# Pinning one VectorE instruction, the fallback's mask, to the middle of phase one

## The chip, the cores and the metric

The kernel runs on one core of a Trainium2 chip. The core has five engines with an instruction stream each: TensorE (PE in the profile, its weight loads are PEld), VectorE (DVE), ScalarE (ACT), GpSimd (POOL) and SyncE (SP), which here only issues DMAs. The metric is the device time of one execution in microseconds (us). The kernel before took 1256.52 us, the median of three runs (1255.74 to 1257.02).

## What is computed

Two independent layers work on inputs of 2048 rows by 1024, and their outputs stand side by side in the result (2048 by 2048, bf16).

Part A is a diagonal complex state-space layer. Its recurrence over the 2048 rows is a complex scan per state:

```python
Lam_bar = jnp.exp(dt * Lam)
B_bar = ((Lam_bar - 1.0) / Lam)[:, None] * Bmat
Bu = jnp.einsum('bld,pd->blp', x + 0j, B_bar)
for t in range(L):
    h = Lam_bar[None, :] * h + Bu[:, t, :]
y = 2.0 * jnp.einsum('blp,dp->bld', hseq, Cmat).real + x * Dskip[None, None, :]
```

Part B is attention with a recurrent memory: 64 segments of 32 rows, each with 8 memory rows in front, 32 heads of 128. The memory of a segment is the first 8 rows of the output of the segment before.

```python
for s in range(n_seg):
    h = jnp.concatenate([mem, xs], axis=1)
    q, k, v = (jnp.einsum('btd,dhe->bhte', h, W) for W in (Wq, Wk, Wv))
    scores = jnp.where(mask, q @ k.T * scale, -1e9)
    o = jnp.einsum('bhte,hed->btd', softmax(scores) @ v, Wo)
    mem = o[:, :M, :]
    outs.append(o[:, M:, :])
```

The mask lets row i see column j where i < 8 or i >= j.

## The kernel before

**The plan.** The kernel guesses the memory rows of all segments from averages, computes all segments at once, and at the end checks the guess (`check`, line 790). Only if the check fails does a branch run `general`, the fallback, which goes through the 64 segments one after another. With these inputs the branch is not taken. The fallback needs a small mask of its own, `k.fmask` (40 by 2 by 40, f32): plane 0 is the 0/1 mask, plane 1 is (plane 0 - 1) * 1e9, to be added to the scores. Nothing but `general` reads it.

**The stages on TensorE.** Phase one (0 to about 343 us) alternates the value projections of part B (`v_x`: 8 head blocks by 4 quarters of the rows) with the input side of part A (`stage1`: 8 blocks of states by 4 blocks of rows, 32 units numbered n = 4*pc + q). Phase two, to about 486 us, is the output side of part A and the guess. Phase three, to about 1027 us, interleaves the query and key projections with attention. Phase four is the output projection, with the check inside it.

**The start.** Eight matmuls on zeros (`warm`) come first. Then `v_x(0, 0)`, the first 512 rows: four tiles of x (128 rows each) arrive untransposed in `b_xr`; for each tile TensorE makes eight transposes into a PSUM buffer psU (two such buffers), and `turn_x0` copies them into `b_xe`, on VectorE for tiles 0 and 2 and on ScalarE for tiles 1 and 3 (`k.copy("vs"[i % 2], ...)`, line 410; the copy itself shows as L89 on VectorE and L87 on ScalarE). TensorE's order is: transposes of tiles 0 and 1; the products of tiles 0 and 1 with the first 128 columns of Wv; transposes of tile 2; the rest of tiles 0 and 1; transposes of tile 3; the whole product of tile 2 (eight matmuls of 512 columns), then of tile 3, this one into a psU buffer. After that come two small transpositions for part A's parameters (`a_r`) and the memory rows (`a_h`), and the second block's values, `v_x(1, 0)`. All later x chunks come transposed by DMA, issued by SP. The products are copied to `b_vst` (two buffers, mostly by ScalarE) and stored to DRAM by ScalarE's queue.

**A unit of stage 1.** 16 matmuls into psU; VectorE multiplies by a table (L265, which frees the psU buffer), adds (L268), scans (L273) and, after a ScalarE copy, multiplies and adds again (L284, L285, into `a_h`, which SP stores). GpSimd computes the carry into the next unit (L278 to L280). `tables` (L221 to L236) makes the tables for the next block of states, on VectorE and ScalarE.

**Masks.** When the loop reaches n == 12 it calls `masks(k)`, GpSimd's masks for attention (lines 112 to 149), and `check_consts(k)`, which builds `k.skip` and `k.fmask`: three GpSimd instructions for plane 0 (L930, L931, L933) and one VectorE instruction for plane 1 (L934).

**What sets the order.** The program is written in one order, but the framework draws the order on each engine itself, by a modelled schedule in which an instruction may go as soon as its inputs are ready. Semaphores are put in afterwards. Exceptions are named by hand: `keep_in_program_order(ins)` adds an order-only edge from the instruction that was written just before `ins` for the same engine. In phase one every TensorE instruction and every DMA of SP is so pinned (`k.pin`); VectorE, ScalarE and GpSimd are not. From phase two on TensorE is free (`k.pin.remove("PE")`), from phase three on SP too. So an instruction without much to wait for, written at n == 12, can stand far ahead of that place in its engine's stream.

Of the kernel before, what the change touches and what calls it, by code (L numbers as in the profile page):

```python
# [12 lines left out]
ALU = mybir.AluOpType  # L13
# [907 lines left out]
def check_consts(k):  # L921

    V, G = k.V, k.G
    k.skip = k.cst.tile([128, 1], FP32, name="c_skip")
    G.memset(k.skip[:], 0.0)
    for r in (2, NTL - 2, NTL - 1):
        G.affine_select(out=k.skip[:], in_=k.skip[:], compare_op=ALU.not_equal, fill=1.0, base=-r,  # L927
                        pattern=[[0, 1]], channel_multiplier=1)
    k.fmask = k.cst.tile([L, 2, L], FP32, name="f_mask")
    G.memset(k.fmask[:], 1.0)  # L930
    G.affine_select(out=k.fmask[:, 0, :], in_=k.fmask[:, 0, :], compare_op=ALU.is_ge, fill=0.0, base=0,  # L931
                    pattern=[[-1, L]], channel_multiplier=1)
    G.memset(k.fmask[0:M, 0, :], 1.0)  # L933
    V.tensor_scalar(k.fmask[:, 1, :], k.fmask[:, 0, :], 1.0, 1.0e9, ALU.subtract, ALU.mult)  # L934


def steps():
# [31 lines left out]
def kernel_main(tc, A_x, A_Lre, A_Lim, A_Bre, A_Bim, A_Cre, A_Cim, A_logdt, A_Dskip, B_x, B_mem0, B_Wq, B_Wk, B_Wv, B_Wo, out,  # L969
                force=False, dbg=None):  # L970
    with ExitStack() as ctx:
# [16 lines left out]
        with pool("p1x", "right") as p1x, pool("p1", "right", 1) as p1:  # L988
# [28 lines left out]
            for kind, pc, q in order[1:]:  # L1017
# [27 lines left out]
                if n == 12:  # L1045
                    masks(k)
                    check_consts(k)
# [167 lines left out]
```

## Time and profile before

| what | value |
|---|---|
| median of three runs | 1256.52 us |
| the profiled execution | 1256.46 us |
| its span, first to last instruction | 1254.8 us |
| mean granted TensorE clock | 0.997 |
| TensorE busy, 0 to 343.2 us | 335.38 us |
| TensorE busy, 343.2 to 486 us | 141.91 us |
| TensorE busy, 486 to 1027 us | 540.07 us |
| TensorE busy, 1027 to 1255 us | 221.92 us |
| VectorE busy, 100 to 300 us | 90% in the first half, 91% in the second |
| DMA, mean busy share of its engines, 0 to 100 us | 91% |

"Busy" is the time in which at least one instruction of the engine ran; matmuls are pipelined and their ends are modelled. Lines are of kernel.py; a copy or matmul made through a helper carries the helper's line (L62 for every TensorE instruction of the kernel and every DMA of SP, L89 and L87 for copies), so tiles are told apart by the names of output and input. An arrow in brackets at the end of a timeline line gives how long the engine had been idle before the instruction, and what released it.

### The profile page before, as it was taken

What the parts mean: (1) busy time and instruction counts of PE and PEld (TensorE: products, weight loads), DVE (VectorE), ACT (ScalarE), POOL (GpSimd) and SP (SyncE); (2) the same over time, 40 slices, a digit from 0 to 9 for tenths busy, and PEclk for the clock granted to TensorE, in tenths of its full rate; (3) what the DMA queues carried; (4) which work ended last, traced back from release to release, by engine and by line L of the source; (5) the groups of instructions that cost most, each with busy time, mean ns of one, the idle gap of its engine ahead of it and who ended that gap; (6) DMA issues with size and microseconds to landing.
All of it is one profiled execution on the core that took longest, in us unless ns stands there. A gap on an engine that the chain in (4) does not pass through costs nothing.

```text
span 1254.8 us, 20111 instructions
## 1 busy us (share of the span) xinstructions
PE 1239.3 (99%) x8270; PEld 664.9 (53%) x8342; DVE 667.6 (53%) x1246; ACT 263.7 (21%) x631; POOL 273.3 (22%) x407
## 2 busy tenths in 40 slices
PE   8999999999999999999999999999999999999998
PEld 4444444444455555556566656556565654446444
DVE  3688899998811124666666666666666641001000
ACT  3544344443310000111112121112111210000000
POOL 3112322121322220232222232222322220000000
PEclk8999999999999999999999999999999999999999
DMA  9975524564698929245464544545373279507000
GB/s 247 233 184 136 161 96 121 157 149 135 181 327 251 280 93 277 69 89 128 105 147 105 135 111 105 135 96 122 92 160 92 58 218 211 117 18 152 18 17 27
DMA packets 314744, 174.18 MB, mean 139 GB/s; under 512 B 138648, under 2 KB 300048, under 8 KB 314648
## 3 DMA queue, kind: packets, MB, share of 16 engines
q1 hardware_dynamic: 292552, 146.22, 48.4%
q10 hardware_dynamic: 21072, 23.47, 5.7%
q0 software_dynamic: 1024, 3.17, 0.7%
q8 instruction: 66, 1.08, 0.4%
q14 instruction: 30, 0.25, 0.1%
HBM read 87.47 MB, written 52.19 MB: 111 GB/s over the span
## 4 chain that ended last, share of the span: by engine, by line
PE 98%; POOL 1%; issue 1%; ACT 0%; DVE 0%; POOLq 0%; ACTq 0%
PE psP L62 81%; PE psU L62 9%; PE psS L62 3%; PE psO L62 2%; PE psR L62 2%; POOL b_m L639 0%; POOL a_r L163 0%; ACT b_e L636 0%; POOL maskB L123 0%; POOL maskA L123 0%; POOL maskB L122 0%; DVE b_xe L89 0%; POOL c_skip L927 0%; POOL maskB L129 0%; POOL maskA L122 0%
## 5 line engine op out<-in xcount | busy, mean ns | idle before, releaser
L62 PE MATMUL psP<-b_xe,b_wq 128*128 128x480 bf16 (+1 forms) x1280 | 247.8, 342 | 0.1
L62 PE MATMUL psP<-b_xe,b_wk 128*128 128x480 bf16 (+1 forms) x1280 | 247.7, 343 | 0.0
L62 PE MATMUL psP<-b_wv,b_xe 128*128 128x512 bf16 (+2 forms) x1033 | 225.1, 375 | 5.5 <-DVE b_xe L89 4.9
L639 POOL TENSOR_TENSOR b_m<-b_e,maskB 99x396 bf16<-99x396 bf16 x160 | 139.4, 871 | 335.9 <-ACT b_e L636 335.9
L636 ACT ACTIVATE b_e<-psS 99x396 bf16<-99x396 f32 x176 | 88.0, 500 | 534.5 <-PE psS L62 526.9
L62 PEld LDWEIGHTS <-b_wk 128*128 128x128 bf16 x1280 | 119.3, 98 | 94.5
L62 PEld LDWEIGHTS <-b_xe 128*128 128x128 bf16 x1056 | 102.7, 99 | 125.3 <-DVE b_xe L89 4.6
L62 PEld LDWEIGHTS <-b_wq 128*128 128x128 bf16 x1280 | 118.5, 98 | 88.1
L89 DVE CAST b_k<-psP 128x480 bf16<-128x480 f32 (+1 forms) x192 | 98.1, 532 | 100.6 <-PE psP L62 100.6
L89 DVE CAST b_q<-psP 128x480 bf16<-128x480 f32 (+1 forms) x192 | 98.1, 532 | 93.9 <-PE psP L62 92.1
L62 PEld LDWEIGHTS <-b_ol 128*128 128x128 bf16 x864 | 84.3, 98 | 94.4
L62 PE MATMUL psU<-a_xT,a_bt 128*128 128x512 bf16 x493 | 113.9, 379 | 1.1
L62 PE MATMUL psP<-t,a_hl 128*128 128x512 bf16 x496 | 112.1, 379 | 0.8
L89 DVE CAST b_ost<-psP 128x512 bf16<-128x512 f32 (+1 forms) x17 | 11.5, 676 | 183.4 <-PE psP L62 182.4
L62 PE MATMUL psP<-wo,b_ol 128*128 128x512 bf16 (+1 forms) x440 | 91.9, 364 | 0.4
L62 PE MATMUL psP<-t,b_ol 128*128 128x512 bf16 x408 | 91.7, 379 | 0.4
L87 ACT ACTIVATE b_vst<-psP 128x512 bf16<-128x512 f32 x126 | 72.3, 591 | 80.0 <-PE psP L62 74.5
L278 POOL TENSOR_SCALAR a_tt<-a_pr,a_tabf 128x1 f32<-128x1 f32 x48 | 34.0, 709 | 250.8 <-DVE a_pr L273 250.8
L656 DVE TENSOR_TENSOR b_ob<-psO,b_accR 99x384 bf16<-99x384 f32 x160 | 85.9, 553 | 2.2
L265 DVE TENSOR_TENSOR a_pr<-psU,a_tabf 128x2048 f32<-128x2048 f32 x32 | 73.0, 2282 | 16.3 <-PE psU L62 14.6
L62 PEld LDWEIGHTS <-a_bt 128*128 128x128 bf16 x512 | 49.2, 98 | 57.6
L62 PEld LDWEIGHTS <-a_hl 128*128 128x128 bf16 x512 | 49.1, 98 | 56.6
(198 smaller groups left out, 965.0 us busy)
## 6 DMA issues: line engine op xcount, KB each, us to landing
b_v<-b_vx SPq DMA_DIRECT2D x16, 1064.2 KB
b_wv<-in_B_Wv_dram SPq DMA_DIRECT2D x16, 1024.0 KB
b_on<-b_ob SPq DMA_DIRECT2D x15, 960.0 KB
b_vx<-b_vst ACTq DMA_DIRECT2D x24, 516.0 KB
a_hs<-a_h SPq DMA_DIRECT2D x32, 256.0 KB
b_wog<-in_B_Wo_dram SPq DMA_DIRECT2D x4, 2048.0 KB
b_wq<-in_B_Wq_dram SPq DMA_DIRECT2D x16, 512.0 KB
b_wk<-in_B_Wk_dram SPq DMA_DIRECT2D x16, 512.0 KB
```

The costliest lines, as they stand in the source:

```text
L62: r = f(*a, **kw)
L87: self.S.activation(out, in_, ACT.Copy)
L89: self.V.tensor_copy(out, in_)
L265: V.tensor_tensor(pr[:], u[:].unsqueeze(1).to_broadcast([128, 2, 2, TB]), view(t3, [[TB + 1, 2], [TB + 1, 2], [1, TB]]), ALU.mult)
L278: G.tensor_scalar(tt[:, j:j + 1], w[:, j, TB - 1:TB], t3[:, 1, TB:TB + 1], None, ALU.mult)
L636: k.S.activation(e[:], s[0:GW], ACT.Exp, scale=float(E) ** -0.5, accum_out=self.accE[0:GW, i:i + 1])
L639: k.G.tensor_tensor(m[:, 0:4 * GW].rearrange("p (a b q) -> p a b q", a=2, b=2), e[:], mask[0:GW, :, :].unsqueeze(2).to_broadcast([GW, 2, 2 ...
L656: V.tensor_tensor(self.ob[:, b0:b0 + n, :], o[0:GW, 0:n, 0:E], r.unsqueeze(2).to_broadcast([GW, n, E]), ALU.mult)
```

## The change

The one VectorE instruction of `check_consts` is handed to `keep_in_program_order`. What was written before it for VectorE is the last instruction of `stage1` for n == 12, the add into `a_h` (L285); the order edge comes from there. The instruction itself, its operands and the GpSimd instructions that it reads from stay as they are.

```diff
@@ -931,7 +931,7 @@
     G.affine_select(out=k.fmask[:, 0, :], in_=k.fmask[:, 0, :], compare_op=ALU.is_ge, fill=0.0, base=0,
                     pattern=[[-1, L]], channel_multiplier=1)
     G.memset(k.fmask[0:M, 0, :], 1.0)
-    V.tensor_scalar(k.fmask[:, 1, :], k.fmask[:, 0, :], 1.0, 1.0e9, ALU.subtract, ALU.mult)
+    k.tc.keep_in_program_order(V.tensor_scalar(k.fmask[:, 1, :], k.fmask[:, 0, :], 1.0, 1.0e9, ALU.subtract, ALU.mult))
```

## The prediction, made before the change was run

> **What bounds the kernel now.** First the page: busy time by engine, the slices, the chain that ended last, the costliest groups.
>
> ```profile
> PE 1239.3 (99%) x8270; PEld 664.9 (53%) x8342; DVE 667.6 (53%) x1246; ACT 263.7 (21%) x631; POOL 273.3 (22%) x407
> ...
> PEclk8999999999999999999999999999999999999999
> ...
> PE 98%; POOL 1%; issue 1%; ACT 0%; DVE 0%; POOLq 0%; ACTq 0%
> ...
> L62 PE MATMUL psP<-b_wv,b_xe 128*128 128x512 bf16 (+2 forms) x1033 | 225.1, 375 | 5.5 <-DVE b_xe L89 4.9
> ```
>
> TensorE is busy 1239.3 of 1254.8 us and carries 98% of the chain; only 15.5 us are not matmul. So an edit on VectorE counts only where TensorE waits for VectorE. The last line names such a place (4.9 us), and the clock row is below full in the first slice alone. Next, who waited for whom (total, times, longest, in us):
>
> ```profile
> DVE f_mask L934 <- POOL f_mask L933: 8.3, 1, 8.3
> ...
> PE psP L62 <- DVE b_xe L89: 4.9, 1, 4.9
> ```
>
> The instruction that is pinned is itself a wait: VectorE stood 8.3 us before it. TensorE's only long wait in the whole span is for a VectorE copy of b_xe. The order of time in the first 32 us shows that they are one event:
>
> ```profile
> 6.37 0.42 DVE L210 CAST a_jf<-a_k 128x513 f32<-128x513 int32 x1
> ...
> 10.86 0.61 PE L62 MATMUL psU<-ident,b_xr 128*128 128x128 bf16 x8
> ...
> 11.50 1.02 ACT L87 ACTIVATE b_xe<-psU 128x1024 bf16<-128x1024 bf16 x1 [0.72 <-PE psU L62]
> ...
> 15.09 0.18 DVE L934 TENSOR_SCALAR f_mask<-f_mask 40x40 f32<-40x40 f32 x1 [8.30 <-POOL f_mask L933]
> 15.19 0.68 DVE L89 COPY b_xe<-psU 128x1024 bf16<-128x1024 bf16 x1
> 15.79 0.68 DVE L89 CAST b_vst<-psP 128x512 bf16<-128x512 f32 x1
> 15.92 0.13 PEld L62 LDWEIGHTS <-b_xe 128*128 128x128 bf16 x2 [4.63 <-DVE b_xe L89]
> 16.32 3.19 PE L62 MATMUL psP<-b_wv,b_xe 128*128 128x512 bf16 x7 [4.86 <-DVE b_xe L89]
> ...
> 19.31 2.69 PE L62 MATMUL psU<-b_wv,b_xe 128*128 128x512 bf16 x8
> ...
> 21.93 0.18 PE L62 MATMUL psR<-ident,a_r 24*128 24x24 bf16 x1
> ```
>
> GpSimd builds its masks from 5.17 to 15.06 us. VectorE holds the mask instruction until the last of them, and the copy of x tile 2 into b_xe is queued behind it. That tile's transposes start at 8.66 and last 0.61 us, so the copy could have run at about 9.3. TensorE finishes the transposes of tile 3 at 11.47 and has nothing until the copy. Last, the clock around the hole (per stretch: busy us of PE, PEld, DVE, ACT, POOL; then PEclk, DMA share, GB/s):
>
> ```profile
> 11.00:11.50 0.50, 0.47 (x9) 0.29 (x6) 0.00 (x0) 0.00 (x0) 0.36 (x5) 1.00 1.10 378
> ...
> 13.50:14.50 1.00, 0.00 (x0) 0.00 (x0) 0.00 (x0) 0.00 (x0) 0.86 (x8) 0.80 0.95 213
> 14.50:15.50 1.00, 0.00 (x0) 0.00 (x0) 0.41 (x2) 0.00 (x0) 0.49 (x4) 0.50 2.23 175
> ...
> 16.30:19.50 3.20, 3.18 (x8) 1.21 (x8) 0.16 (x1) 0.00 (x0) 0.00 (x0) 0.50 1.06 223
> ...
> 21.00:22.00 1.00, 1.00 (x7) 0.34 (x6) 0.00 (x0) 0.00 (x0) 0.00 (x0) 1.00 1.27 289
> ```
>
> The hole costs twice: the wait, and a clock that falls to 0.50 in it and is back only near 20.8 us.
>
> **What the Trainium skill says.** "TensorE: Matmul & The Clock Gate", Part 1: an idle window of about 3.4 us halves the clock and about 3.4 us of work restores it. The trace agrees: the fall is inside the 4.4 us hole, the recovery some 4.9 us after the restart at 15.9. Same page, Architectural detail: VectorE's queue is strict FIFO. The copy behind the mask shows that. "SBUF — State Buffer", two separate sides: VectorE and GpSimd can block each other on a shared port pair. The copy will now run while GpSimd builds masks, so this matters; the same copy at 5.76 us, beside GpSimd's work, took 692 ns against 675 at 15.19 with GpSimd idle. I take no loss.
>
> **The change, part by part.** The pin adds an order edge: the mask comes after the VectorE instruction traced before it, which is the sum into a_h (L285) of the 13th stage-1 unit (n = 12).
>
> (a) *The wait goes.* The record at 16.32 has seven of eight matmuls; eight half-rate ones of 427 ns (3.19 us for 7 and a bit) back from 19.31 begin at 15.89. So TensorE's hole is 11.46 to 15.89 = 4.43 us. What is late next? Tile 2's copy would end at about 9.35 + 0.69 = 10.0, before 11.46. Tile 3's copy, on ScalarE, ends at 12.52 and is needed only after tile 2's eight matmuls, at 13.2. The psU buffer for tile 3's product is freed by tile 2's copy at 10.0. So the hole is gone: 4.43 us.
>
> (b) *The slow clock goes.* The 16 matmuls for tiles 2 and 3 run from 15.89 to 21.93 = 6.04 us. At full rate 32 such matmuls take 6.91 us on the chain, 0.216 each: 3.46 us. Saved 2.58 us. Sum (a)+(b): 7.01 us; the a_r transposition would start at 11.46 + 3.46 = 14.92 instead of 21.93.
>
> (c) *What now comes 7 us earlier must be there.* DMA does not move with TensorE: it is near saturation until 60 us. Bytes counted from the span's start put the three MB of x tiles and Wv before 11.5 us (the rate falls from 378 to 282 GB/s there), so block 1's Wv, needed at 15.2, has arrived. SP issues the transposed x chunks of b_xe and a_xT back to back; from the GB/s rows I estimate that they land about 15, 24 (a_xT 0), 29, 34, 40, 49 and 54 us. Their uses, 7 us earlier than now, fall at 22.1, 35.9, 39.5, 46.4, 56.7, 60.2 and 67.5. The least slack is about 7 us. Two or three of ScalarE's 516 KB stores fall earlier among them, some 1 MB or 4 us at 240 GB/s: still covered. From 60 us SP's loads follow a_h and buffers, which shift with TensorE. I charge nothing; if the cover fails, 1 to 3 us come back.
>
> (d) *The mask in its new place.* 177 ns on VectorE. GpSimd was done at 15.06, so no wait. Its neighbours now, on VectorE:
>
> ```profile
> 173.09 0.68 DVE L285 TENSOR_TENSOR a_h<-a_n 128x1024 bf16<-128x1024 bf16 x1
> 173.69 2.28 DVE L265 TENSOR_TENSOR a_pr<-psU,a_tabf 128x2048 f32<-128x2048 f32 x1
> ```
>
> Behind it is the product of unit 13, which frees a psU buffer at 175.97; TensorE needs that buffer for unit 15 at 188.73. The cover is 12.8 us against 0.18, and VectorE itself waits for TensorE at 192.38. Cost 0, at most 0.18. If GpSimd's mask work were also moved there (9.9 us ahead of the carries that the scans need), the cover would still hold it. No DMA is moved; SP is passed by nothing.
>
> (e) *After phase one.* Past the first five microseconds TensorE has no other wait over 0.4 us, so the shift should arrive at the end whole.
>
> Sum: the profiled execution, 1256.46 us (span 1254.8 and 1.7 around it), becomes 1249.45, span 1247.8. It lies 0.06 below the median 1256.52, so the median becomes 1249.5.
>
> **Rivals.**
> 1. *A transfer takes the wait's place*: Wv of block 1, or the first store of b_vst, which ScalarE's later copies into that buffer wait for. For: DMA is full. Against: the byte count. Gives back about 2 us: 1251.5.
> 2. *Only the hole goes, the clock is low anyway*, because some 3 us of idleness stay: 4.4 us off, 1252.1. Against: (a) finds no second releaser after 11.46 us.
> 3. *The pin does not do it*: another instruction waiting for GpSimd is placed early on VectorE. Only a_jf reads GpSimd there, and it is already past at 6.79: 1256.5.
> 4. *Slower*: the framework orders unpinned instructions by a modelled schedule; a shift of the start redraws the order in attention, where TensorE is not pinned. Each of 176 score units waits for ScalarE and GpSimd; with 0.08 us more per unit TensorE loses 14 us and the end is 1263.5. It decides from 7.0/176 = 0.04 us per unit. For: 160 mask products of 871 ns stand in that loop. Against: TensorE is 100.00 busy in each 100 us of it, so the order has reserve.
>
> **How the numbers follow.** Forecast 0.80; rivals 0.09, 0.03, 0.03, 0.05. The time is the forecast's: 1249.5. Its own spread is that of the three runs, 0.8 below and 0.5 above, plus 0.18 for (d) and about 0.3 for the copy's start; the range runs on through rival 1: 1248.4 to 1251.8. No change means within 0.2%, 2.5 us, about what a measurement can tell. Faster: forecast and rivals 1 and 2, 0.92; same 0.03; slower 0.05.
>
> **What would show it.** VectorE's 8.3 us wait for f_mask absent; the b_xe copy near 9.4; no TensorE hole at 11.5; clock 1.00 from 12 to 22 us; the a_r transposition near 14.9; L934 near 167 us, with no idle before it; unit 0 of stage 1 near 36.0 instead of 43.0. It is wrong if TensorE waits for a DMA before 70 us, if the clock falls at about 13 us all the same, or if attention shows new waits.

## The result and the profile after

| kernel | median, us | range, us | runs |
|---|---|---|---|
| before | 1256.49 | 1255.74 to 1257.02 | 6 |
| after | 1250.43 | 1249.00 to 1254.56 | 6 |

The ratio is 0.9958, with a 95% interval of 0.9941 to 0.9976. The gain is 6.1 us, where 7.0 was forecast, and the times now spread over 5.6 us, where before they spread over 1.3. The experiments below trace both differences mainly to one wait, and the profiled execution, 1253.39 us (span 1251.6), is one of those that it touched. First the page of the changed kernel: busy time, clock, chain, and the group that had waited for b_xe.

```profile
PE 1241.9 (99%) x8342; PEld 664.0 (53%) x8342; DVE 667.9 (53%) x1246; ACT 263.5 (21%) x631; POOL 273.3 (22%) x407
...
PEclk9999999999999999999999999999999999999999
...
PE 98%; DMA 1%; ACT 1%; POOL 0%; DVE 0%; issue 0%; ACTq 0%
...
L62 PE MATMUL psP<-b_wv,b_xe 128*128 128x512 bf16 (+2 forms) x1048 | 226.1, 375 | 2.7 <-ACT b_vst L87 2.4
```

The clock row has lost its 8. In the chain that ended last GpSimd (POOL) has gone from 1% to 0%, and DMA has come in with 1%. The value projections still wait, but for ScalarE's copy into b_vst, and no longer for VectorE's copy of b_xe. The start in order of time (start, duration, engine, line, work, count; in brackets the idle time before and its releaser):

```profile
8.95 0.69 DVE L89 COPY b_xe<-psU 128x1024 bf16<-128x1024 bf16 x1 [2.16 <-PE psU L62]
10.50 0.61 PE L62 MATMUL psU<-ident,b_xr 128*128 128x128 bf16 x8
...
10.95 1.89 PE L62 MATMUL psP<-b_wv,b_xe 128*128 128x512 bf16 x8
12.67 1.89 PE L62 MATMUL psU<-b_wv,b_xe 128*128 128x512 bf16 x8
...
14.49 0.18 PE L62 MATMUL psR<-ident,a_r 24*128 24x24 bf16 x1
```

The copy of tile 2 runs at 8.95 (before 15.19), the products of tiles 2 and 3 follow the transposes of tile 3 without a hole and at full rate, and the a_r transposition starts at 14.49 instead of 21.93: 7.44 us earlier. Then, from the order of time in the stretch from 20 to 48 us:

```profile
23.73 6.00 SPq L62 DMA_TRANSPOSE b_xe<-in_B_x_dram  x1
...
25.17 0.37 ACTq L493 DMA_DIRECT2D b_vx<-b_vst  x1
...
29.81 0.39 ACTq L493 DMA_DIRECT2D b_vx<-b_vst  x1
...
35.76 1.09 ACT L87 ACTIVATE b_vst<-psP 128x512 bf16<-128x512 f32 x2 [5.37 <-DMA b_vx<-b_vst]
36.41 3.53 PE L62 MATMUL psP<-b_wv,b_xe 128*128 128x512 bf16 x8 [2.40 <-ACT b_vst L87]
...
39.78 3.62 PE L62 MATMUL psU<-a_xT,a_bt 128*128 128x512 bf16 x16
```

ScalarE issues the second store of b_vst, that of `v_x(1, 0)`, at 25.17. The fourth block of values needs the same buffer (there are two), ScalarE stands 5.37 us until the store has landed, the PSUM buffers stay full, and TensorE stands 2.40 us. Unit 0 of stage 1 begins at 39.78, against 43.01 before: of the 7.44 us won, 3.23 are left, which is the difference of the spans (3.2). The chain of waits, shown over 25 to 50 us, has the store in it:

```profile
25.17 10.51 DMA b_vx<-b_vst
...
35.76 0.61 ACT b_vst L87
36.41 3.53 PE psP L62 x8
```

The stretches around it (per stretch: busy us of PE, PEld, DVE, ACT, POOL; PEclk, DMA share, GB/s) show that this wait, too, costs more than its length:

```profile
34.00:35.00 1.00, 0.01 (x1) 0.00 (x0) 0.00 (x0) 0.00 (x0) 0.00 (x0) 1.00 1.14 188
35.00:36.00 1.00, 0.00 (x0) 0.00 (x0) 0.00 (x0) 0.24 (x1) 0.00 (x0) 1.00 1.20 185
36.00:37.00 1.00, 0.59 (x2) 0.25 (x2) 0.00 (x0) 1.00 (x3) 0.00 (x0) 0.68 1.18 201
37.00:38.00 1.00, 1.00 (x3) 0.29 (x2) 0.51 (x1) 1.00 (x3) 0.00 (x0) 0.50 1.28 290
```

The clock falls to 0.50 once more. Eight matmuls take 3.37 us (36.41 to 39.78) where eight at full rate take 1.73: 1.64 us on top of the 2.40. Last, VectorE around the pinned instruction:

```profile
169.85 0.69 DVE L285 TENSOR_TENSOR a_h<-a_n 128x1024 bf16<-128x1024 bf16 x1
170.45 0.19 DVE L934 TENSOR_SCALAR f_mask<-f_mask 40x40 f32<-40x40 f32 x1
170.56 2.27 DVE L265 TENSOR_TENSOR a_pr<-psU,a_tabf 128x2048 f32<-128x2048 f32 x1
```

It stands where the edit put it, with no idle time before it. On VectorE it is the only instruction whose place in the order changed; TensorE, GpSimd and SP have the same order as before, and on ScalarE two neighbours, a copy for the scan (L274) and a copy of products (L87), changed places.

### The profile page after: what moved, and what is told of

Its sections match the earlier page's. It is cut to its first block, busy times and chain, and to the rows that moved or that the text cites. A ratio compares the mean times of both kernels' runs of the same rounds, so it can differ in the third digit from the quotient of the medians.

```text
span 1251.6 us, 20183 instructions
## 1 busy us (share of the span) xinstructions
PE 1241.9 (99%) x8342; PEld 664.0 (53%) x8342; DVE 667.9 (53%) x1246; ACT 263.5 (21%) x631; POOL 273.3 (22%) x407
## 3 DMA queue, kind: packets, MB, share of 16 engines
q0 software_dynamic: 1024, 3.17, 0.8%
## 4 chain that ended last, share of the span: by engine, by line
PE 98%; DMA 1%; ACT 1%; POOL 0%; DVE 0%; issue 0%; ACTq 0%
PE psP L62 81%; PE psU L62 9%; PE psS L62 3%; PE psO L62 2%; PE psR L62 2%; DMA b_vx<-b_vst 1%; POOL b_m L639 0%; ACT b_vst L87 0%; ACT b_e L636 0%; ACT L185 0%; DVE b_xe L89 0%; ACT a_fr L234 0%; ACT a_k L231 0%; ACT a_tabf L229 0%; ACT a_k L227 0%
## 5 line engine op out<-in xcount | busy, mean ns | idle before, releaser
L87 ACT ACTIVATE b_vst<-psP 128x512 bf16<-128x512 f32 x126 | 72.2, 591 | 76.7 <-PE psP L62 69.8
```

Of the source, the lines that this page charges most:

```text
L87: self.S.activation(out, in_, ACT.Copy)
```

## The experiments

Two events can be read off in every profile: the start of the a_r transposition, which shows what the hole and the slow clock cost, and the start of stage 1's unit 0, which shows what was given back in between. "Given back" is the interval between the two less 21.07 us, its length wherever TensorE does not wait for a b_vst copy. "Waits" are TensorE's idle times for that copy before unit 0 (in warm_third the first is for the same copy into a buffer of a_pr).

| kernel | a_r, us | unit 0, us | given back | waits | profiled, us | profiled less unit 0 |
|---|---|---|---|---|---|---|
| before | 21.93 | 43.01 | 0.01 | none | 1256.46 | 1213.45 |
| after | 14.49 | 39.78 | 4.22 | 2.40 | 1253.39 | 1213.61 |
| again | 14.37 | 35.44 | 0 | none | 1248.85 | 1213.41 |
| again2 | 14.50 | 37.61 | 2.04 | 1.87 | 1251.94 | 1214.33 |
| third | 14.79 | 35.86 | 0 | none | 1249.37 | 1213.51 |
| third2 | 14.51 | 35.59 | 0.01 | none | 1249.10 | 1213.51 |
| early | 14.64 | 36.91 | 1.20 | 1.03 | 1250.38 | 1213.47 |
| poolq | 14.63 | 36.76 | 1.06 | 0.89 | 1250.46 | 1213.70 |
| warm20 | 19.46 | 42.54 | 2.01 | 1.51, 0.40 | 1256.01 | 1213.47 |
| warm_third | 19.71 | 42.71 | 1.93 | 1.52, 0.29 | 1256.11 | 1213.40 |
| mid_third | 20.91 | 41.98 | 0 | none | 1255.47 | 1213.49 |
| dose | 19.96 | 41.03 | 0 | none | 1254.50 | 1213.47 |
| split | 14.90 | 39.81 | 3.84 | 1.99 | 1253.31 | 1213.50 |
| plain | 14.45 | 43.70 | 8.18 | 1.95, 4.27 | 1258.48 | 1214.78 |

The last column is the same within 0.3 us for twelve of the fourteen: in these the end follows from the first 44 us. In plain the slow clock lasts through unit 0, which takes 4.90 us instead of 3.62. In again2 the wait for a b_vst copy comes once more at the end of phase one: TensorE stands 0.74 us until 347.61, behind a store that was issued at 338.04 and took 8.84 us, and this accounts for most of the 0.9 us.

Why does the store land late? Three explanations were open: that its queue is served only behind SP's queue (Q in the texts on record); that a transposing load in particular holds it up (T); or that the traffic as such does (B).

**again and again2: the changed kernel once more.** No edit; again ran beside third, again2 on another chip beside third2.

> The changed kernel once more, for a second profile and the spread of its time. Theory S (the start is 7.4 us earlier, and a varying part comes back because ScalarE waits for the store of the second block of values, b_vst, before it can fill that buffer again): times between 1249.0 (no wait) and 1254.6 as before, and in the profile the TensorE wait for ScalarE's b_vst copy near 34 us plus the half-rate matmuls after it account for the difference to 1249.0 within 0.4 us. Rival M (the spread comes from the mask's new place or from a later stage): the first 45 us are alike in both profiles of the changed kernel, and the difference shows later.

> The changed kernel, on the same chip as the run with the plain loads and with the third buffer, to compare spreads. 1248.9 to 1254.6; the profile, if its time is above 1249.5, shows TensorE's wait for the b_vst copy near 34 us of the size that is missing.

again: median 1249.05 us (1248.85 to 1250.21), ratio 0.9942 [0.9929, 0.9956]. again2: 1250.88 us (1249.68 to 1252.81), ratio 0.9958 [0.9945, 0.9971]. The same program, with the same instructions in the same order, has the wait in one profile and lacks it in another. The order of time of again, 20 to 48 us:

```profile
24.49 7.00 SPq L62 DMA_TRANSPOSE b_xe<-in_B_x_dram  x1
25.04 0.44 ACTq L493 DMA_DIRECT2D b_vx<-b_vst  x1
...
31.79 1.09 ACT L87 ACTIVATE b_vst<-psP 128x512 bf16<-128x512 f32 x2 [1.53 <-DMA b_vx<-b_vst]
...
35.44 3.62 PE L62 MATMUL psU<-a_xT,a_bt 128*128 128x512 bf16 x16
```

The store is issued within 0.13 us of the time that it had in the profile of after, but ScalarE goes on at 31.79 instead of 35.76. TensorE's PSUM buffers cover this: no wait, and unit 0 is at 35.44, 7.57 us earlier than before. Of the 4.54 us between the two profiled times, 4.34 lie before unit 0.

**third and third2: a third staging buffer.** The third block of values, `v_x(0, 1)`, is put into a buffer of its own, so that the fourth needs the buffer of the first store and not of the second.

```diff
             b.stage_init()
+            b.st2 = p1.tile([128, 4, 4, EV], BF16, name="a_pr", bufs=2)
+            k.G.memset(b.st2[:, :, :, E:EV], 1.0)
...
-        st = self.next_st()
+        st = self.st2 if (hb, q) == (0, 1) else self.next_st()
```

> The changed kernel with a third staging buffer for the third block of values (it borrows a buffer of a_pr, idle until 39 us), so that the fourth block waits for the first block's store and not for the second's. Theory S: the wait is gone in every execution, 1249.0 to 1249.5 with a spread under 1 us. Rival M: same spread and median as the changed kernel, about 1250.5. Rival D (DMA itself is late, whichever buffer waits): a wait for a transposed load or for the first store takes its place, 1250 to 1254.

> The changed kernel with the third staging buffer, beside the changed kernel on the same chip. If the buffer takes the varying part away: 1249.3 to 1249.7 with a spread under 0.5 us whatever the changed kernel does here. If the chip decides: as the changed kernel.

third: 1249.52 us (1249.37 to 1249.65), ratio 0.9943 [0.993, 0.9957]. third2: 1249.35 us (1249.10 to 1249.55), ratio 0.9946 [0.9933, 0.9959]. From the order of time of third2:

```profile
24.40 6.57 SPq L62 DMA_TRANSPOSE b_xe<-in_B_x_dram  x1
...
25.19 0.37 ACTq L493 DMA_DIRECT2D b_vx<-b_vst  x1
...
29.82 0.37 ACTq L493 DMA_DIRECT2D b_vx<-a_pr  x1
...
35.59 3.62 PE L62 MATMUL psU<-a_xT,a_bt 128*128 128x512 bf16 x16
```

TensorE has no wait for a b_vst copy, and the spread shrinks from 3.1 us (again2, same chip) to 0.45. So the varying part of the loss before unit 0 goes through the staging buffer: that is shown. On the chip of third2 it beats both kernels (1249.35 beside 1250.88 for the change and 1256.55 for before; the ranges do not overlap); on that of third it is level with the change (1249.52 and 1249.05) and has only the narrower spread.

**early: the wait removed in another way.** On the kernel before, without the pin, `check_consts` is written ahead of `masks`, so GpSimd serves its three instructions first.

```diff
-                    masks(k)
                     check_consts(k)
+                    masks(k)
```

> The kernel before, without the pin, with GpSimd's mask for the fallback written ahead of the attention masks instead of behind them. The mask instruction stays early on VectorE, but what it reads is done near 6.5 us instead of 15.1. If only the length of its wait matters, this is as the changed kernel: 1249.0 to 1254.6, median about 1250.4, with the a_r transposition near 14.5 us. If it is its presence ahead of the copy that matters: 1256.5.

1250.18 us (1249.54 to 1251.52), ratio 0.9949 [0.9935, 0.9962]. L934 runs at 6.70 on VectorE with no wait, ahead of the copy of tile 2, and the a_r transposition at 14.64 is within 0.3 us of after. So the harm came from the length of the wait and not from the instruction's presence early in VectorE's stream. The store returns here too (1.03 us of waiting).

**mid_third and dose: a shorter wait.** Both write `check_consts` into the middle of `masks` on the kernel before, without the pin: mid_third half way, together with the third buffer, dose ahead of the last quarter (the diff shown).

```diff
-    for m, ns in ((k.maskA[:, 0, :], 2), (k.maskA[:, 1, :], 3), (k.maskB[:, 0, :], 3), (k.maskB[:, 1, :], 3)):
+    mB1 = k.maskB[:, 1, :]
+    for m, ns in ((k.maskA[:, 0, :], 2), (k.maskA[:, 1, :], 3), (k.maskB[:, 0, :], 3), (mB1, 3)):
+        if ns == 3 and m is mB1:
+            check_consts(k)
...
-                    check_consts(k)
```

> The kernel before without the pin, with the third staging buffer, and the fallback's mask written in the middle of GpSimd's attention masks: it should be ready near 13 us, 2 us before the kernel before has it. VectorE's copy of tile 2 then ends near 14 us and TensorE's hole is some 2.6 to 3.0 us instead of 4.4 to 5. If the clock's fall is a separate price paid only by long idleness (it fell at 13.5 to 14.5 us): 1249.4 + 2.8 = 1252.2 with the clock up, or up to 1254.8 if it falls all the same. If time followed the presence of the wait alone: 1256.5.

> The kernel before without the pin, with the fallback's mask ahead of the last quarter of GpSimd's attention masks: ready near 13.4 us instead of 15.1. VectorE's wait is then about 6.7 us instead of 8.3 and TensorE's hole 1.6 us shorter. If the price of the wait is the hole plus half rate after it, the a_r transposition comes at 20.3 us (clock fallen) or at 17.9 (clock still up) instead of 21.9; the median follows by 1.6 to 4.0 us, less what ScalarE's stores take back: 1252.5 to 1256.0.

mid_third missed: the framework kept the last of the three GpSimd instructions at the end, VectorE waited 8.32 us until 14.99, and the time was 1256.05 us (1255.24 to 1256.93), ratio 1.0002 [0.9994, 1.0011]. It serves as a control: the third buffer alone gains nothing while the hole is there. (In its profile the clock came back a microsecond sooner than in before, so a_r is at 20.91; the median does not show it.) In dose the mask ran at 13.93, 1.16 us earlier than before; 1253.92 us (1252.73 to 1255.63), ratio 0.9981 [0.9974, 0.9987]. TensorE's matmuls and the clock in dose, from the order of time and from the stretches:

```profile
15.16 3.14 PE L62 MATMUL psP<-b_wv,b_xe 128*128 128x512 bf16 x7 [3.90 <-DVE b_xe L89]
18.13 1.89 PE L62 MATMUL psU<-b_wv,b_xe 128*128 128x512 bf16 x8
19.96 0.18 PE L62 MATMUL psR<-ident,a_r 24*128 24x24 bf16 x1
```

```profile
14.00:15.00 1.00, 0.00 (x0) 0.13 (x2) 1.00 (x3) 0.00 (x0) 0.85 (x12) 0.85 2.04 76
15.00:16.00 1.00, 0.84 (x2) 0.30 (x2) 0.30 (x1) 0.00 (x0) 0.39 (x3) 0.50 0.43 91
...
18.00:19.00 1.00, 1.00 (x6) 0.39 (x4) 0.00 (x0) 0.60 (x1) 0.00 (x0) 0.94 1.09 245
```

The first eight matmuls are slow and the next eight are not (1.89 us for eight), while before the next eight were still partly slow (2.69). The a_r transposition comes 1.97 us earlier for 1.16 us of wait removed; the other 0.8 is the shorter slow stretch. Nothing is given back, and unit 0 comes 1.98 us earlier. The twenty times fall into three groups: ten from 1252.73 to 1253.35, seven near 1254.5, among them the profiled one, and three near 1255.6. The median lies in a gap between them, so the account holds for the middle group; the fast half has no profile.

**warm20 and warm_third: the clock alone.** The hole stays, but 20 matmuls whose result nobody reads keep TensorE busy in it. This is extra work; nothing is left out. warm_third adds the third buffer.

```diff
             self.turn_x0(3)
+            pd = k.ps("R")
+            for _ in range(20):
+                k.PE.matmul(pd[:], w[:, 0, 0:128], w[:, 0, :], start=True, stop=True)
```

> The kernel before, with the mask where it was, and 20 matmuls on Wv (result unused, extra work) in the hole behind tile 3's transposes, so that the clock stays up while VectorE waits. If the price of the wait is 4.4 us of hole and 2.6 us of half-rate matmuls, the second part alone comes back: 1253.9. Rival: the half rate costs nothing, since the matmuls after the hole would wait for data anyway: 1256.5. If the matmuls outlast the hole: up to 0.5 us above.

> The 20 matmuls in the hole (extra work, result unused) together with the third staging buffer, so that no store can take back what the clock gives. If the half-rate matmuls after the hole cost 2.5 us, and only ScalarE's wait for the store hid that in the run without the buffer: 1254.0, spread under 1 us. If the loss in that run had another cause: 1255.7 again.

The clock part is as expected: the 16 matmuls for tiles 2 and 3 run at full rate, and a_r comes at 19.46, 2.47 us earlier (2.58 in the prediction). The time is a miss: 1255.72 us (1254.60 to 1256.49), ratio 0.9992 [0.9984, 1.0001]. Of the 2.47 us, 2.01 are given back. warm_third was to show that this is the staging buffer; it missed too: 1255.45 us (1255.04 to 1256.12), ratio 0.9995 [0.9986, 1.0003]. Its order of time says why:

```profile
23.61 5.94 SPq L62 DMA_TRANSPOSE b_xe<-in_B_x_dram  x1
...
32.98 1.58 ACT L87 ACTIVATE a_pr<-psP 128x512 bf16<-128x512 f32 x3 [2.10 <-DMA b_xe<-in_B_x_dram]
33.62 7.07 PE L62 MATMUL psP<-b_wv,b_xe 128*128 128x512 bf16 x32 [1.52 <-ACT a_pr L87]
```

ScalarE's copy goes into a fresh buffer, and yet it comes after 2.10 us of idling for SP's load of b_xe, which it does not read. Ahead of it in ScalarE's stream is the issue of the second store, at 32.56 where it could have gone at about 30.4. warm20 has the same picture (issue at 32.24, ScalarE idle 2.09 us). So the loss here begins with a store that is issued late, and everything behind it on ScalarE comes late with it. That the issue waits for the load rests on the releaser that the profile names; why it should (a completion semaphore that the two transfers share is a guess) is not shown.

**poolq: the stores from GpSimd's queue.** The changed kernel, with the stores of the first four blocks issued by GpSimd.

```diff
-        Q = k.nc.scalar
+        Q = k.nc.gpsimd if hb < 2 and q < 2 else k.nc.scalar
```

> The changed kernel, with the stores of the first four blocks of values issued by GpSimd instead of ScalarE's queue. Theory Q (the second store cannot start while SP's transposing load of a whole chunk, 6 us, is being issued, because both hardware queues are served one behind the other): through GpSimd's queue the store starts within 2 us of its issue, the wait near 31 us is gone, 1249.0 to 1249.5. Theory B (the store is slow because the DMA engines are full): it lands as late as before, 1249.0 to 1254.6 with the same spread.

1249.38 us (1249.21 to 1250.46), ratio 0.9949 [0.9935, 0.9962]. In its profile the second store is issued at 24.85 and moves its first bytes in the stretch from 28 to 29; ScalarE waits 3.17 us for it. It lands 9.45 us after its issue. A store on GpSimd's software queue is late as well, so explanation Q fails as it was put; that this queue has a reason of its own for being late was not tested. Whether this version spreads less than after cannot be told from five runs.

**split and plain: other loads around the store.** split cuts the transposing load of the third x chunk (issued at 23.73 in after) into four of 128 rows. plain puts four untransposed loads that SP would issue later ahead of it.

```diff
-            return [(64 + 512 * q, 512 * q, 512)]
+            return [(64 + 512 * q + 128 * i, 512 * q + 128 * i, 128) for i in range(4)] if q == 2 else [(64 + 512 * q, 512 * q, 512)]
```

```diff
+                if len(loads) == 3 and kind == "v":
+                    next(sx)
                 if loads and kind == "v":
...
-                if n == 1:
-                    next(sx)
```

> The changed kernel, with the transposing load of the third x chunk cut into four of 128 rows. Theory Q: the second store starts behind a 1.5 us piece instead of a 6 us one, moves its first bytes near 27 us and lands before ScalarE needs the buffer at 30.3: 1249.0 to 1249.5, spread under 1 us. Theory B: no difference to the changed kernel, or slower if small transposes move less per us.

> The changed kernel with SP's order altered: the four plain loads of x rows for the averages (1 MB, issued at 57 us in the changed kernel) go ahead of the third transposing load of x, so that the second store is issued beside plain loads instead of 1 to 1.5 us behind a transposing one. Theory T (a store that is issued behind a transposing load waits until that load's data are through): the store's first bytes within 2.7 us of its issue, ScalarE not stalled over 1 us for it, 1249.0 to 1249.5. Theory B (any load of 1 MB in front of it is as bad): the store lands as late as in the changed kernel, 9 to 10 us after its issue, and the time is 1250 or more.

Both missed. split: 1253.31 us (1251.45 to 1254.88), ratio 0.9976 [0.9969, 0.9984]. plain: 1255.69 us (1251.58 to 1260.83), ratio 0.9995 [0.9987, 1.0003]. The order of time of plain:

```profile
27.89 0.37 ACTq L493 DMA_DIRECT2D b_vx<-b_vst  x1
28.36 1.58 ACT L87 ACTIVATE b_vst<-psP 128x512 bf16<-128x512 f32 x3 [2.74 <-DMA b_xr<-in_B_x_dram]
29.00 7.07 PE L62 MATMUL psP<-b_wv,b_xe 128*128 128x512 bf16 x31 [1.95 <-ACT b_vst L87]
...
39.69 1.09 ACT L87 ACTIVATE b_vst<-psP 128x512 bf16<-128x512 f32 x2 [7.11 <-DMA b_vx<-b_vst]
40.34 3.57 PE L62 MATMUL psP<-b_wv,b_xe 128*128 128x512 bf16 x8 [4.27 <-ACT b_vst L87]
```

The store's issue now comes late itself (at 27.89, with ScalarE idle for 2.74 us; in split at 28.37, with 2.78 us), and the profile names a load as releaser, of b_xr here and of b_xe in split. In plain its landing holds ScalarE a second time, for 7.11 us, and the clock falls in that wait; in split it falls after the first. Because the issue moved, neither run tells T from the traffic. What plain shows is the size of the stake: with VectorE's wait gone, a change in the order of SP's loads alone gives the whole gain back (8.18 us of the 7.48 won at a_r).

## Why the prediction was right, and where it was not

- **(a) and (b), the hole and the clock: 7.01 us forecast, 7.44 measured in after.** The two were separated at the a_r transposition: the clock is worth 2.47 us there (warm20, forecast 2.58), so the hole is the rest, about 5.0. That the 2.47 us by themselves shorten the whole kernel was not seen, because 2.0 of them went back before unit 0. Most of the 0.43 us between forecast and measurement is not the change: the transposes of tile 3 start at 10.50 in after and at 10.86 in before, 0.36 us apart, and over all profiles that start varies between 10.37 and 10.90. The copy of tile 2 beside GpSimd's masks took 0.69 us: no loss there, as forecast.
- **(c), the transfers that must be there 7 us earlier: charged at nothing; this term was mis-sized.** Before unit 0 it cost 0 (again), 2.04 (again2) and 4.22 us (after) in the three profiles of the changed kernel, and in again2 another 0.9 us at 347 us. The step named "1 to 3 us" if the cover fails. The loads of x and Wv were there in time, as computed: TensorE waits for no load in this stretch of after. What the step left out: it counted the stores as bytes only, while a store must have landed before its buffer is free, and the landing is not a matter of bytes alone (in after the store's bytes had not begun to move although the core moved only 0.02 MB from 26.5 to 28.4 us). It also priced the wait without the slow clock that rides on it, 1.8 us in after.
- **Rival 1 was the thing that happened, in part of the runs.** It named the first store; it is the second one. It said 1251.5 us, with a loss of about 2. Of the sixteen runs of the changed kernel twelve lie at or below 1251.43, inside the range that was given (1248.4 to 1251.8), and four above that range, up to 1254.56. So the forecast of 1249.5 describes the runs without the wait; that the median of the first six, 1250.43, came within 1 us of it is in part luck, since it depends on how many of the six had the wait.
- **(d), the mask in its new place: 0, as forecast.** 0.19 us on VectorE at 170.45, and no wait for it in the list of waits. "L934 near 167 us" was for a full shift of 7 us; here 3.2 us arrived, and the product behind it, at 173.69 before, is at 170.56.
- **(e), the shift arrives whole: right** from unit 0 on, by the last column of the table, with the one exception at 347 us in again2.
- **Rivals 2, 3 and 4 fell.** The clock stays at 1.00 from 11 to 22 us, through the place of the old hole, the pin holds, and TensorE has no new wait in attention.
- **The signs named in advance:** the copy of b_xe near 9.4 (8.95), a_r near 14.9 (14.49), unit 0 near 36.0 (35.44 in again, 39.78 in after). "Wrong if TensorE waits for a DMA before 70 us" came true by way of ScalarE, and the view of TensorE's waits names the copy and not the store behind it: the DMA shows one line further up, with ScalarE.

What stays open is why one and the same store takes 6.7 us to land in one execution (again) and 10.5 in another (after). Q fails as it was put, by poolq; T and the traffic as such were not told apart. How to free the store's issue from the load that it seems to wait for was not tried.

## What to carry to other kernels

When an early wait goes, look at every buffer that is reused soon after, and ask not only whether its loads have come but whether the store out of it has landed; a third buffer at that one place took the spread from 3.1 to 0.45 us. A queue's in-order stream hides dependences: a cheap instruction placed early on VectorE, or a store's issue on ScalarE, holds up everything behind it for as long as it waits itself (here 8.30 us and 2.1 to 2.8 us). Before believing a median, profile the same kernel more than once: two profiles of this one differ by 4.5 us, and comparing them named the next bottleneck.

## What was not expected of the hardware

**A store stood for up to 5.8 us before its first bytes moved.** The DMA queues of after in three stretches (queue and kind: packets, MB, share of the engines): 25 to 30, 30 to 31 and 31 to 36 us.

```profile
q1 hardware_dynamic: 2745, 0.70, 116.1%
...
q10 hardware_dynamic: 2, 0.00, 0.6%
...
q10 hardware_dynamic: 1047, 1.05, 91.1%
```

The first line is SP's queue; ScalarE's, q10, moved nothing from 25 to 30 us although its store was issued at 25.17, two packets by 31, and then two whole stores in five microseconds. The stretch in between was not busy throughout: from 26.5 to 28.4 the core moved 0.02 MB. The Trainium skill, "DMA: Bandwidth & Descriptors", under queues, rings and completion order, says that a DMA engine goes round the queues for which it has work, packet by packet. By that one would look for the store's packets beside those of the load. These windows do not show them, even while the engines moved next to nothing; whether the store's work had reached the engines by then, the trace does not tell. The distance from the load does not settle the delay either: where the store was issued 0.55 us after the load (again), its first bytes came 2.5 us later; at 1.3 us (early) 4.1, at 1.4 (after) 5.8, at 1.6 (again2) 5.6, but at 1.9 (third) 4.0.

**The clock falls after less idle time than expected.** The same page as in the prediction, "TensorE: Matmul & The Clock Gate", Part 1, gives an idle window of about 3.4 us. In the kernel before, the prediction took its trace to agree; but the granted clock of 0.80 in the stretch from 13.5 to 14.5 us, if it steps from 1.00 to 0.50, puts the fall at about 14.1, some 2.6 us after TensorE's last work. A wait of 2.40 us (after) and one of 1.99 (split) were followed by matmuls at half rate, for 1.8 us of loss on top of each; in split the clock fell only about a microsecond after work had begun again. Waits of 1.95 (plain, the first), 1.87 (again2) and 1.52 us (warm_third) were not, and the last two cost their own length and 0.1 to 0.2 us. Near 2 us a wait in this kernel about doubles its price. 1.99 and 1.95 us lie so close together that the length alone may not decide; that was not tested.
